# In the last network, sums of two products go to SBUF, and ScalarE squares the positive parts while it rounds them

## The chip, the cores and the metric

The kernel runs on one NeuronCore of one Trainium2 chip. Its engines have an instruction queue each and work through it in order: TensorE (matmuls, into PSUM), VectorE, ScalarE, GpSimd and SyncE; the profile calls them PE, DVE, ACT, POOL and SP. An instruction waits at the head of its queue until the instructions of other engines that it needs have signalled. The metric is the device time of one execution in microseconds. The kernel before takes 709.72 us (median of 3 runs, 708.33 to 710.09).

## The reference

Three networks run one after another on 1152 tokens of 512 values, all in 32-bit floats: causal attention with a bias (2 batches, 8 heads, 576 positions), a mixture of four ReLU networks (weights of 512 x 1024 and 1024 x 512 each), and a last network with a squared ReLU:

```python
# the four experts, then the last network
for e in range(E):
    h = np.maximum(x @ w1[e], 0.0)
    out += p[:, e:e + 1] * (h @ w2[e])
...
h = x @ w_in          # (1152, 512) @ (512, 2048)
r = np.maximum(h, 0.0)
g = r * r
return (g @ w_out).astype(np.float32)
```

## The kernel before

Each matmul is made in three parts: a value x is split into hi, x rounded to the matmul format fp32r, and lo, x minus hi, and the products hi*hi, hi*lo and lo*hi are added up in PSUM. So each value that goes into a matmul costs an instruction that rounds it and one that subtracts.

The code at hand is the long stage that makes the second to fourth expert and the last network. It runs over 20 pieces of hidden columns (q, 0 to 19; four for each 1024 columns; q from 12 on is the last network) and two blocks of tokens (b: 512 tokens as two halves of 256, 640 tokens as two halves of 320). One call of `group` handles one q and one b; there are 40, and they are numbered here from 0 in the order of the list `groups` (L1125). Group 24 is the first of the last network, group 26 is piece 12 with the tokens of 320 columns a half, group 27 piece 13 with the same tokens.

A group makes its four quarters of hidden values (j is the half of the columns, half the half of the tokens) from seven block products instead of eight (Winograd's form of Strassen's method). The products are made in the order 1, 2, 6, 5, 7, 4, 3, each by six matmuls (`product`, L1017). Products 1, 6, 7 and 4 add up in one PSUM bank, pa, and between them ScalarE copies the running sum out into SBUF (`keep`, L1064: tiles u1 and u2). Product 2 has the bank pb. Products 5 and 3 share one bank, pc, one after the other. pa and pb change places from group to group, and pc is a single bank for all groups.

`hidden(j, half, ps, kept)` (L1069) makes a quarter out of a bank and a kept sum. VectorE adds the two: for j = 0 in place, in the bank, for j = 1 into the kept tile. For q below 12 ScalarE then writes hi with a Relu, and VectorE writes lo with one scalar_tensor_tensor (positive part minus hi). In the last network the value is squared, with four instructions in turn: ScalarE's Relu into a tile r (L1081), VectorE's scalar_tensor_tensor r = max(x, 0) * r (L1082), which reads x again, ScalarE's copy of r to hi (L1083), and VectorE's r minus hi to lo (L1084). The bank is free when the last of these that reads x is done.

`y_unit` (L1035) is the second matmul of the network: for one tile of 128 tokens, six matmuls of 512 columns, out of a group's hi and lo. The units of a group are issued in between the products of the next one, so that TensorE has work while the other engines make hidden values. After every second piece VectorE adds the bank of a tile to the accumulator in SBUF (L240, L242).

Between the products, `do_next` also issues other work: sums and splits of the weights (`w_pair`, L943; ScalarE's copies L970, L971, L985 and L992, GpSimd's differences L79), and the decoding of the last network's weights, which arrive in another number format (`decode`, L120): ScalarE's L132, GpSimd's L134, then five instructions on VectorE, L141, L145, L147, L149 and L150, and a store.

The order in each engine's queue isn't the order of this code: a scheduler sets it when the program is built, by its own estimate of when each instruction can start. So the change of one buffer or one instruction can move many others. Tiles come from pools with a number of buffers (`bufs`): a new tile of a name waits until all use of the one that had its buffer is over.

Of the kernel before, what the change touches and what calls it, by code (L numbers as in the profile page):

```python
# [8 lines left out]
F32 = mybir.dt.float32  # L9
F32R = mybir.dt.float32r  # L10
U32 = mybir.dt.uint32
AF = mybir.ActivationFunctionType
ALU = mybir.AluOpType
# [3 lines left out]
P = 128  # L17
# [3 lines left out]
E = 4  # L21
# [27 lines left out]
def fused_kernel(ctx, tc, qk, v, s, dp, w1, w2, wi, wo, out):  # L49
# [5 lines left out]
    nc = tc.nc  # L55
# [130 lines left out]
    def ph_tile():  # L186
        pool = ph_pools[ph_count[0] % len(ph_pools)]
        ph_count[0] += 1
        return pool.tile([P, 512], F32, tag="ph", name="ph")
# [76 lines left out]
    class Unit:  # L266
        def __init__(self, b, h, q0, q1, group, slot):
            self.b, self.h, self.q0, self.q1 = b, h, q0, q1
            self.group, self.slot = group, slot
            kt = KT[b]  # L270
            self.tiles = [i for i in range(5) if kt[i] >= q0 and kt[i + 1] <= q1]
# [29 lines left out]
    with tc.tile_pool(name="att", bufs=2) as att, tc.tile_pool(name="atc", bufs=1) as const_a:  # L301
# [107 lines left out]
        for u in units:  # L409
            for i in u.tiles:  # L410
                t = Step()
# [464 lines left out]
    str_p = ctx.enter_context(tc.tile_pool(name="str", bufs=1))  # L876
# [140 lines left out]
    def product(ps, i, q, b, first):  # L1017
        wn, xn = PRODUCT[i]
        n = BLOCKS[b][1]
        s, c0, stride = W_AT[wn]  # L1020
        m = 0
        for k2 in range(2):
            for wh, xx in ((0, 0), (0, 1), (1, 0)):
                c = c0 + k2 * stride
                nc.tensor.matmul(  # L1025
                    ps[:, :n],
                    lhsT=pw[q][s][:, wh, c : c + P],
                    rhs=x_part(b, xn, xx, k2),
                    start=(first and m == 0),
                    stop=(m == 5),  # L1030
                    skip_group_check=True,
                )
                m += 1
# [19 lines left out]
    def group(q, b, turn, do_next):  # L1053

        n = BLOCKS[b][1]
        hs = [str_p.tile([P, 2, 640], F32R, tag="h", name="h", bufs=4) for _ in range(2)]
        free = [ph_tile(), ph_tile()]  # L1060
        pa, pb = free if turn else free[::-1]
        pc = pc_p.tile([P, 512], F32, tag="y", name="pc")

        def keep(ps, name):  # L1064
            t = str_p.tile([P, 320], F32, tag=name, name=name, bufs=1)
            nc.scalar.copy(t[:, :n], ps[:, :n])  # L1066
            return t

        def hidden(j, half, ps, kept):  # L1069
            x = ps[:, :n]  # L1070
            if kept is not None:
                x = kept[:, :n] if j else x
                nc.vector.tensor_tensor(x, ps[:, :n], kept[:, :n], op=ALU.add)
            cols = slice(half * n, half * n + n)
            hi, lo = (hs[j][:, i, cols] for i in range(2))
            if q < E * 4 - 4:
                nc.scalar.activation(hi, x, AF.Relu)
                nc.vector.scalar_tensor_tensor(lo, x, 0.0, hi.bitcast(F32), op0=ALU.max, op1=ALU.subtract)  # L1078
                return
            r = str_p.tile([P, 320], F32, tag="r", name="r", bufs=2)[:, :n]  # L1080
            nc.scalar.activation(r, x, AF.Relu)  # L1081
            nc.vector.scalar_tensor_tensor(r, x, 0.0, r, op0=ALU.max, op1=ALU.mult)  # L1082
            nc.scalar.copy(hi, r)  # L1083
            nc.vector.tensor_tensor(lo, r, hi.bitcast(F32), op=ALU.subtract)  # L1084

        product(pa, 1, q, b, True)
        p1 = keep(pa, "u2")
        product(pb, 2, q, b, True)
        hidden(0, 0, pb, p1)
        do_next(0)  # L1090
        product(pa, 6, q, b, False)
        u1 = keep(pa, "u1")
        product(pc, 5, q, b, True)
        do_next(1)
        product(pa, 7, q, b, False)
        u2 = keep(pa, "u2")
        hidden(1, 1, pc, u2)
        do_next(2)
        product(pa, 4, q, b, False)
        hidden(1, 0, pa, None)  # L1100
        do_next(3)
        product(pc, 3, q, b, False)
        hidden(0, 1, pc, u1)
        do_next(4)
        t0 = BLOCKS[b][0] // P
        order = range(t0, t0 + 2 * n // P)
        if (q + 2) // 4 == E - 1 and (q + 2) % 4 < 2:
            order = LAST[b]
        return [lambda t=t: y_unit(q, b, t, hs) for t in order]
# [72 lines left out]
    for i, (q, b) in enumerate(groups):  # L1182
        todo = units
        n_units, n_side = len(todo), len(side[i])
        done = [0, 0]

        def do_next(k):

            upto = min(n_units, k if n_units == 4 and k == 3 else k + 1)
            while done[0] < upto:  # L1190
                todo[done[0]]()
                done[0] += 1
            while done[1] < n_side * (k + 1) // 5:
                side[i][done[1]]()
                done[1] += 1
            for op in extra[i, k]:
                op()

        units = group(q, b, i % 2, do_next)
# [50 lines left out]
```

## Time and profile before

| | |
|---|---|
| median of 3 runs | 709.72 us (708.33 to 710.09) |
| the profiled execution | 707.28 us, its span 705.5 us |
| TensorE busy | 685.7 us (97%), 4164 matmuls |
| VectorE busy | 500.9 us (71%) |
| ScalarE busy | 353.1 us (50%) |
| GpSimd busy | 315.3 us (45%) |
| chain that ended last | TensorE 76%, VectorE 14% |
| first and last squared Relu of the last network (L1081) | 500.1 and 694.5 us |
| granted clock of TensorE | 1.00 in every stretch from 100 to 650 us |

The times of the trace are microseconds from the start of the span. The stage with the groups begins at about 210 us, the last network at about 498 us. A row of a timeline gives an instruction's start and its length; a bracket says how long the engine had been idle before it and which instruction ended that. Rows of several equal instructions are merged with a count. For TensorE the ends of matmuls are modelled, so two of them overlap in the listing: how long a block takes is read from the distance of its start to the next one's.

### The profile page before, as it was taken

What the parts mean: (1) busy time and instruction counts of PE and PEld (TensorE: products, weight loads), DVE (VectorE), ACT (ScalarE), POOL (GpSimd) and SP (SyncE); (2) the same over time, 40 slices, a digit from 0 to 9 for tenths busy, and PEclk for the clock granted to TensorE, in tenths of its full rate; (3) what the DMA queues carried; (4) which work ended last, traced back from release to release, by engine and by line L of the source; (5) the groups of instructions that cost most, each with busy time, mean ns of one, the idle gap of its engine ahead of it and who ended that gap; (6) DMA issues with size and microseconds to landing.
All of it is one profiled execution on the core that took longest, in us unless ns stands there. A gap on an engine that the chain in (4) does not pass through costs nothing.

```text
span 705.5 us, 11939 instructions
## 1 busy us (share of the span) xinstructions
PE 685.7 (97%) x4164; PEld 598.1 (85%) x4164; DVE 500.9 (71%) x1142; ACT 353.1 (50%) x880; POOL 315.3 (45%) x332
## 2 busy tenths in 40 slices
PE   9889999999999999999999999999998999999997
PEld 8668787778998989889989899889997888899996
DVE  5986677751668657887787887869588789955464
ACT  7976776651355343352533433535574445535341
POOL 5754454420073583591770943812438726704000
PEclk9999999999999999999999999999999999999999
DMA  7652333100141234243343433431203332300012
GB/s 224 201 154 77 104 86 86 36 1 1 60 148 36 75 116 140 100 150 120 121 154 115 134 121 119 150 120 46 60 31 106 96 120 83 103 18 1 1 60 75
DMA packets 37060, 66.17 MB, mean 94 GB/s; under 512 B 4392, under 2 KB 12232, under 8 KB 37000
## 3 DMA queue, kind: packets, MB, share of 16 engines
q1 hardware_dynamic: 27784, 40.23, 19.1%
q10 hardware_dynamic: 9216, 25.17, 10.7%
q8 instruction: 33, 0.54, 0.3%
q14 instruction: 27, 0.22, 0.1%
HBM read 52.73 MB, written 10.82 MB: 90 GB/s over the span
## 4 chain that ended last, share of the span: by engine, by line
PE 76%; DVE 14%; issue 4%; ACT 3%; POOL 1%; ACTq 0%; DVEq 0%; POOLq 0%
PE y L1043 26%; PE ph L1025 16%; PE ph L197 7%; PE pc L1025 7%; PE y L223 6%; PE o L616 4%; PE pt L559 3%; DVE dy L145 3%; DVE raw_d L149 2%; PE s L463 2%; DVE raw_d L141 2%; PE s L464 1%; PE idle L337 1%; DVE h L1078 1%; ACT w L992 1%
## 5 line engine op out<-in xcount | busy, mean ns | idle before, releaser
L1043 PE MATMUL y<-w,h 128*128 128x512 f32 x1080 | 276.3, 392 | 0.0
L1043 PEld LDWEIGHTS y<-w,h 128*128 128x128 f32 x1080 | 193.9, 188 | 30.9
L1025 PE MATMUL ph<-tx,w 128*128 128x256 f32 (+1 forms) x720 | 115.4, 296 | 0.1
L1025 PEld LDWEIGHTS ph<-tx,w 128*128 128x128 f32 x720 | 106.2, 189 | 7.6 <-ACT u L1066 0.9
L1066 ACT COPY u<-ph 128x256 f32<-128x256 f32 (+1 forms) x120 | 47.7, 397 | 94.8 <-PE ph L1025 93.0
L79 POOL TENSOR_TENSOR w<-raw_w,w 128x512 fp32r<-128x512 f32 x58 | 80.7, 1405 | 18.1 <-ACT w L992 18.1
L1025 PE MATMUL pc<-xh,w 128*128 128x256 f32 (+1 forms) x320 | 78.4, 300 | 6.6 <-DVE r L1082 3.1
L1025 PE MATMUL ph<-xh,w 128*128 128x256 f32 (+1 forms) x320 | 77.9, 298 | 1.3 <-DVE h L1078 0.8
L79 POOL TENSOR_TENSOR w<-val,w 128x512 fp32r<-128x512 f32 x40 | 58.7, 1483 | 43.8 <-ACT w L985 43.8
L519 POOL TENSOR_SCALAR p<-p,stat 128x128 f32<-128x128 f32 (+9 forms) x80 | 47.7, 608 | 56.3 <-DVE stat L514 21.4
L134 POOL TENSOR_SCALAR dy<-dy 128x512 f32<-128x512 f32 x32 | 19.9, 622 | 114.8 <-ACT dy L132 107.5
L1025 PEld LDWEIGHTS pc<-xh,w 128*128 128x128 f32 x320 | 56.0, 188 | 11.2 <-DVE r L1082 4.6
L1025 PEld LDWEIGHTS ph<-xh,w 128*128 128x128 f32 x320 | 56.0, 188 | 4.5 <-DVE h L1078 1.5
L197 PE MATMUL ph<-xh,w 128*128 128x256 f32 (+1 forms) x256 | 58.3, 301 | 0.1
L223 PE MATMUL y<-w,h 128*128 128x512 f32 x216 | 57.4, 396 | 0.0
L501 ACT ACTIVATE p<-p,stat 128x384 f32<-128x384 f32 (+9 forms) x80 | 46.6, 583 | 18.8 <-DVE stat L487 15.9
L1025 PE MATMUL ph<-xl,w 128*128 128x256 f32 (+1 forms) x160 | 47.4, 297 | 0.0
L1025 PE MATMUL pc<-xl,w 128*128 128x256 f32 (+1 forms) x160 | 47.3, 296 | 0.0
L487 DVE CUSTOM_DVE_ANT_0 p<-s,mask 128x448 f32<-128x448 f32 (+8 forms) x72 | 33.1, 462 | 19.4 <-PE pt L559 12.2
L1084 DVE TENSOR_TENSOR h<-r,h 128x256 fp32r<-128x256 f32 (+1 forms) x64 | 36.1, 567 | 13.9 <-ACT h L1083 12.5
L197 PEld LDWEIGHTS ph<-xh,w 128*128 128x128 f32 x256 | 43.3, 188 | 1.6 <-DVE h L211 0.4
L223 PEld LDWEIGHTS y<-w,h 128*128 128x128 f32 x216 | 38.9, 188 | 6.0
(149 smaller groups left out, 1273.2 us busy)
## 6 DMA issues: line engine op xcount, KB each, us to landing
raw_w<-in_w SPq DMA_DIRECT2D x64, 256.0 KB
raw_d<-in_wi ACTq DMA_DIRECT2D x16, 512.0 KB
staged<-dy ACTq DMA_DIRECT2D x32, 256.0 KB
raw_d<-in_wo ACTq DMA_DIRECT2D x16, 512.0 KB
raw_w<-staged SPq DMA_DIRECT2D x32, 256.0 KB
raw<-in_qk SPq DMA_DIRECT2D x40, 144.0 KB
v<-in_v SPq DMA_DIRECT2D x8, 256.0 KB
out<-acc_a SPq DMA_DIRECT2D x6, 256.0 KB
```

The lines of the kernel that those rows point to most:

```text
L79: eng.tensor_tensor(out_, a, b.bitcast(F32), op=ALU.subtract)
L145: nc.vector.scalar_tensor_tensor(top, top, 0x80000000, high, op0=ALU.bitwise_and, op1=ALU.bitwise_or)
L197: nc.tensor.matmul(ps[:, :n], lhsT=w1_ap(e, wh, kk, f), rhs=x[:, kk, t0 : t0 + n], start=(i == 0), stop=(i == 3 * KD - 1),)
L223: mm = nc.tensor.matmul(ps, lhsT=h[:, hh, o : o + P], rhs=w2_ap(e, wh, f), start=(f == 0 and i == 0), stop=(f == NF - 1 and i == 2),)
L487: t.red = nc.vector.tensor_tensor_reduce(t.p[: t.n, a:z], ps[: t.n, : z - a], t.bias[:, a:z], scale=-0.125, scalar=init, op0=ALU.add, op1= ...
L501: t.exp = nc.scalar.activation(t.p[: t.n, : t.w], t.p[: t.n, : t.w], AF.Exp, bias=t.nmax, scale=-1.0, accum_out=t.st[: t.n, 4 + t.c : 5 + ...
L519: norm = nc.gpsimd.tensor_scalar(t.p[: t.n, : t.w], t.p[: t.n, : t.w], t.st[: t.n, 6 + t.c : 7 + t.c], 1.0, op0=ALU.mult, op1=ALU.mult)
L616: return nc.tensor.matmul(u.o[i * D : (i + 1) * D, qs - u.q0 : u.nq], lhsT=vv[:kn, j, i * D : (i + 1) * D], rhs=rhs, start=(j == 0), stop= ...
L1025: nc.tensor.matmul(ps[:, :n], lhsT=pw[q][s][:, wh, c : c + P], rhs=x_part(b, xn, xx, k2), start=(first and m == 0), stop=(m == 5), skip_gr ...
L1043: nc.tensor.matmul(ps, lhsT=hs[j][:, hh, o : o + P], rhs=wt[e, 2, g][:, wh, j * DM : (j + 1) * DM], start=(g % 2 == 0 and i == 0 and j == ...
L1066: nc.scalar.copy(t[:, :n], ps[:, :n])
L1084: nc.vector.tensor_tensor(lo, r, hi.bitcast(F32), op=ALU.subtract)
```

## The change

Three things change in `group`, the first two only in the last network (`late`) except for the number of buffers.

- The sum of product 3 and u1 (half 1, j = 0) goes into the kept tile u1, not back into the bank; the sum of product 2 and the first kept sum (half 0) stays in its bank as before, and that of product 5 and u2 goes to u2 as before. For half 1 the squares are then made in the kept tile itself; for half 0 in the tile r.
- ScalarE writes hi as the Square of r, straight after its Relu; VectorE then makes r * r, both inputs from r, instead of max(x, 0) * r, and subtracts hi.
- u1 has two buffers instead of one, for all groups, and r one instead of two. The four tiles take the same space as before.

```diff
--- before.py
+++ after.py
@@ -1061,26 +1061,32 @@
         pa, pb = free if turn else free[::-1]
         pc = pc_p.tile([P, 512], F32, tag="y", name="pc")
 
+        def kept_tile(name):
+            bufs = 2 if name == "u1" else 1
+            return str_p.tile([P, 320], F32, tag=name, name=name, bufs=bufs)[:, :n]
+
         def keep(ps, name):
-            t = str_p.tile([P, 320], F32, tag=name, name=name, bufs=1)
-            nc.scalar.copy(t[:, :n], ps[:, :n])
+            t = kept_tile(name)
+            nc.scalar.copy(t, ps[:, :n])
             return t
 
         def hidden(j, half, ps, kept):
+            late = q >= E * 4 - 4
             x = ps[:, :n]
             if kept is not None:
-                x = kept[:, :n] if j else x
-                nc.vector.tensor_tensor(x, ps[:, :n], kept[:, :n], op=ALU.add)
+
+                x = kept if (half if late else j) else x
+                nc.vector.tensor_tensor(x, ps[:, :n], kept, op=ALU.add)
             cols = slice(half * n, half * n + n)
             hi, lo = (hs[j][:, i, cols] for i in range(2))
-            if q < E * 4 - 4:
+            if not late:
                 nc.scalar.activation(hi, x, AF.Relu)
                 nc.vector.scalar_tensor_tensor(lo, x, 0.0, hi.bitcast(F32), op0=ALU.max, op1=ALU.subtract)
                 return
-            r = str_p.tile([P, 320], F32, tag="r", name="r", bufs=2)[:, :n]
+            r = x if half else kept_tile("r")
             nc.scalar.activation(r, x, AF.Relu)
-            nc.vector.scalar_tensor_tensor(r, x, 0.0, r, op0=ALU.max, op1=ALU.mult)
-            nc.scalar.copy(hi, r)
+            nc.scalar.activation(hi, r, AF.Square)
+            nc.vector.tensor_tensor(r, r, r, op=ALU.mult)
             nc.vector.tensor_tensor(lo, r, hi.bitcast(F32), op=ALU.subtract)
 
         product(pa, 1, q, b, True)
```

With it the scheduler's order changes, from group 10 on. The three places below are those that the prediction speaks of.

VectorE, groups 11 and 12 (the experts, where the code of a group is as before). L1073, in the new file L1079, is the add of `hidden`; L1078, L1084 in the new file, makes lo; L238 adds to an accumulator; L141 to L149 are decoding. `pc_4124` is group 11's bank pc. Before:

```order
L141 TENSOR_SCALAR raw_d_4088<-dy_4200 128x512
L1073 TENSOR_TENSOR pc_4124<-pc_4124,u1_4155 128x320
L145 SCALAR_TENSOR_TENSOR dy_4200<-dy_4200,raw_d_4088 128x512
L147 TENSOR_SCALAR raw_d_4088<-dy_4200 128x512
L1073 TENSOR_TENSOR ph_4249<-ph_4249,u2_4258 128x256
L149 SCALAR_TENSOR_TENSOR raw_d_4088<-raw_d_4088 128x512
L1078 SCALAR_TENSOR_TENSOR h_4120<-pc_4124,h_4120 128x320
```

Now:

```order
L1079 TENSOR_TENSOR pc_4124<-pc_4124,u1_4155 128x320
L141 TENSOR_SCALAR raw_d_4088<-dy_4200 128x512
L1084 SCALAR_TENSOR_TENSOR h_4120<-pc_4124,h_4120 128x320
L145 SCALAR_TENSOR_TENSOR dy_4200<-dy_4200,raw_d_4088 128x512
L1079 TENSOR_TENSOR ph_4249<-ph_4249,u2_4258 128x256
L238 SCALAR_TENSOR_TENSOR acc_a_75<-y_4142,pn_74,acc_a_75 128x512
L238 SCALAR_TENSOR_TENSOR acc_a_75<-y_4163,pn_74,acc_a_75 128x512
```

The instruction that makes lo out of `pc_4124`, the last that reads the bank, stood behind L141, L145, L147 and L149, and now stands behind L141 alone.

VectorE, group 26. `pc_6109`, now `pc_6105`, is its bank pc, and the add into u2 is that of product 5. Before:

```order
L141 TENSOR_SCALAR raw_d_5493<-dy_6200 128x512
L145 SCALAR_TENSOR_TENSOR dy_6200<-dy_6200,raw_d_5493 128x512
L147 TENSOR_SCALAR raw_d_5493<-dy_6200 128x512
L149 SCALAR_TENSOR_TENSOR raw_d_5493<-raw_d_5493 128x512
L1073 TENSOR_TENSOR u2_6172<-pc_6109,u2_6172 128x320
L150 TENSOR_TENSOR dy_6200<-dy_6200,raw_d_5493 128x512
L1082 SCALAR_TENSOR_TENSOR r_6175<-u2_6172,r_6175 128x320
L1082 SCALAR_TENSOR_TENSOR r_6193<-ph_6108,r_6193 128x320
```

Now (L1079 is the add, L1089 r * r, L1090 makes lo):

```order
L141 TENSOR_SCALAR raw_d_5493<-dy_6195 128x512
L145 SCALAR_TENSOR_TENSOR dy_6195<-dy_6195,raw_d_5493 128x512
L147 TENSOR_SCALAR raw_d_5493<-dy_6195 128x512
L149 SCALAR_TENSOR_TENSOR raw_d_5493<-raw_d_5493 128x512
L150 TENSOR_TENSOR dy_6195<-dy_6195,raw_d_5493 128x512
L1079 TENSOR_TENSOR u2_6168<-pc_6105,u2_6168 128x320
L1079 TENSOR_TENSOR u1_6139<-pc_6105,u1_6139 128x320
L1089 TENSOR_TENSOR u2_6168<-u2_6168 128x320
```

The fifth step of the decoding, L150, stood behind the add into u2 and now stands ahead of it; the two adds follow each other.

ScalarE, same place. `r_6193`, now `r_6188`, is the tile r of product 4 of group 26. Before (L1081 Relu, L1083 copy to hi):

```order
L1081 ACTIVATE r_6193<-ph_6108 128x320
L970 CAST w_6351<-raw_w_6224 128x256
L155 DMA staged5121_6320<-dy_6200 128x512
L1083 CAST h_6106<-r_6175 128x320
L1066 COPY u2_6244<-ph_6235 128x320
L126 DMA raw_d_6322<-in_wo 128x1024
L1083 CAST h_6106<-r_6193 128x320
L132 ACTIVATE dy_6324<-raw_d_5619 128x512
L971 CAST w_6351<-raw_w_6226 128x512
L985 CAST w_6352<-val_6345 128x512
L985 CAST w_6352<-val_6346 128x512
```

Now (L1087 Relu, L1088 Square to hi):

```order
L1088 ACTIVATE h_6102<-u2_6168 128x320
L1087 ACTIVATE r_6188<-ph_6104 128x320
L132 ACTIVATE dy_6317<-raw_d_5619 128x512
L970 CAST w_6344<-raw_w_6218 128x256
L971 CAST w_6344<-raw_w_6220 128x512
L985 CAST w_6345<-val_6338 128x512
L985 CAST w_6345<-val_6339 128x512
L1088 ACTIVATE h_6102<-r_6188 128x320
```

The step that writes hi for product 4 came ahead of L132, L971 and both L985, and now comes behind them and L970.

TensorE, the end of the program. The last `ph` and `pc` rows are products 4 and 3 of group 39; the y tiles fed by `h_7749` and `h_7750`, now `h_7719` and `h_7720`, are that group's. Before:

```order
L1025 MATMUL ph_7751<-tx14_2486,w_7353 128x320 x6
L1025 MATMUL pc_7753<-xh_72,w_7354 128x320
L1025 MATMUL pc_7753<-xl_73,w_7354 128x320
L1025 MATMUL pc_7753<-xh_72,w_7354 128x320 x2
L1025 MATMUL pc_7753<-xl_73,w_7354 128x320
L1025 MATMUL pc_7753<-xh_72,w_7354 128x320
L1043 MATMUL y_7853<-w_7254,h_7642 128x512
L1043 MATMUL y_7774<-w_7494,h_7749 128x512 x3
L1043 MATMUL y_7795<-w_7494,h_7749 128x512 x3
L1043 MATMUL y_7774<-w_7494,h_7750 128x512 x2
L1043 MATMUL y_7795<-w_7494,h_7750 128x512 x2
```

Now:

```order
L1043 MATMUL y_7744<-w_7469,h_7719 128x512 x3
L1043 MATMUL y_7765<-w_7469,h_7719 128x512 x3
L1025 MATMUL ph_7721<-tx14_2486,w_7331 128x320 x6
L1025 MATMUL pc_7723<-xh_72,w_7332 128x320
L1025 MATMUL pc_7723<-xl_73,w_7332 128x320
L1025 MATMUL pc_7723<-xh_72,w_7332 128x320 x2
L1025 MATMUL pc_7723<-xl_73,w_7332 128x320
L1025 MATMUL pc_7723<-xh_72,w_7332 128x320
L1043 MATMUL y_7744<-w_7469,h_7720 128x512 x2
L1043 MATMUL y_7765<-w_7469,h_7720 128x512 x2
L1043 MATMUL y_7744<-w_7469,h_7720 128x512
```

Two tiles' three matmuls each of group 39 and the last one of group 38 stood behind products 4 and 3; now the six stand ahead of them, and what follows product 3 at once reads `h_7720`, the half of the columns that product 4 makes.

## Rows read from the trace of the kernel before

**Rows 1.** The page, busy time of each engine:

```profile
PE 685.7 (97%) x4164; PEld 598.1 (85%) x4164; DVE 500.9 (71%) x1142; ACT 353.1 (50%) x880; POOL 315.3 (45%) x332
```

**Rows 2.** Timeline of TensorE: start, us, instruction; in brackets idle time before, releaser:

```profile
356.57 0.39 PE L1025 MATMUL pc<-xh,w 128*128 128x256 f32 x1 [0.51 <-DVE h L1078]
...
535.76 0.42 PE L1025 MATMUL pc<-xh,w 128*128 128x320 f32 x1 [1.22 <-DVE u L1073]
...
537.30 0.41 PE L1025 MATMUL ph<-xh,w 128*128 128x320 f32 x1 [0.39 <-DVE r L1082]
...
541.05 0.41 PE L1025 MATMUL pc<-xh,w 128*128 128x320 f32 x1 [0.34 <-DVE r L1082]
...
555.78 0.39 PE L1025 MATMUL pc<-xh,w 128*128 128x256 f32 x1 [1.19 <-DVE r L1082]
...
568.74 0.39 PE L1025 MATMUL pc<-xh,w 128*128 128x256 f32 x1 [1.52 <-DVE r L1082]
...
575.29 0.28 PE L1025 MATMUL pc<-xh,w 128*128 128x256 f32 x1
```

**Rows 3.** Timeline of VectorE, 351.7 to 356.5, groups 11 and 12:

```profile
351.75 0.48 DVE L1073 TENSOR_TENSOR pc<-pc,u 128x320 f32<-128x320 f32 x1
352.15 1.38 DVE L145 SCALAR_TENSOR_TENSOR dy<-dy,raw_d 128x512 uint32<-128x512 uint32 x1
...
356.04 0.48 DVE L1078 SCALAR_TENSOR_TENSOR h<-pc,h 128x320 fp32r<-128x320 f32 x1
```

**Rows 4.** Timeline of VectorE, 530.2 to 536.5, group 26:

```profile
530.23 0.69 DVE L240 COPY acc_a<-y 128x512 f32<-128x512 f32 x1 [0.17 <-PE y L1043]
530.83 1.31 DVE L141 TENSOR_SCALAR raw_d<-dy 128x512 uint32<-128x512 uint32 x1
...
534.21 1.10 DVE L149 SCALAR_TENSOR_TENSOR raw_d<-raw_d 128x512 f32<-128x512 uint32 x1
535.23 0.48 DVE L1073 TENSOR_TENSOR u<-pc,u 128x320 f32<-128x320 f32 x1
535.63 0.81 DVE L150 TENSOR_TENSOR dy<-dy,raw_d 128x512 f32<-128x512 f32 x1
```

**Rows 5.** Timeline of ScalarE, 536.4 to 540.2:

```profile
536.44 0.40 ACT L970 CAST w<-raw_w 128x256 fp32r<-128x256 f32 x1
...
537.92 0.68 ACT L132 ACTIVATE dy<-raw_d 128x512 f32<-128x512 f32 x1
538.50 0.60 ACT L971 CAST w<-raw_w 128x512 fp32r<-128x512 f32 x1
539.01 1.14 ACT L985 CAST w<-val 128x512 fp32r<-128x512 f32 x2
```

**Rows 6.** Chain of waits, in order of time: start, us, what:

```profile
651.88 0.72 PE pc L1025 x6
...
692.07 0.88 PE ph L1025 x6
...
693.82 7.06 PE y L1043 x31
```

**Rows 7.** Groups by line and form, 498 to 697: busy, mean ns, idle; then ScalarE's timeline:

```profile
L1084 DVE TENSOR_TENSOR h<-r,h 128x320 fp32r<-128x320 f32 x32 | 22.1, 693 | 10.5 <-ACT h L1083 9.7
...
L1083 ACT CAST h<-r 128x320 fp32r<-128x320 f32 x32 | 14.6, 460 | 12.0 <-DVE r L1082 11.9
...
L1082 DVE SCALAR_TENSOR_TENSOR r<-ph,r 128x320 f32<-128x320 f32 x16 | 7.8, 488 | 11.9 <-ACT r L1081 11.8
...
693.04 0.44 ACT L1081 ACTIVATE r<-ph 128x320 f32<-128x320 f32 x1 [2.72 <-PE ph L1025]
```

**Rows 8.** Busy us (PE, PEld, DVE, ACT, POOL) of two stretches; a group of the second:

```profile
550.00:600.00 50.00, 47.28 (x275) 42.21 (x274) 44.24 (x77) 25.62 (x61) 27.91 (x25) 1.00 0.35 107
650.00:697.00 47.00, 47.00 (x272) 42.35 (x271) 25.32 (x54) 17.63 (x43) 0.00 (x0) 1.00 0.06 23
...
L1084 DVE TENSOR_TENSOR h<-r,h 128x320 fp32r<-128x320 f32 x8 | 3.9, 490 | 2.3 <-ACT h L1083 2.1
```

## The prediction

> **What bounds the kernel now.** I read the busy line of the page first [rows 1]: TensorE is busy 685.7 of 705.5 us, so everything else is a question of when TensorE waits. The change moves no matmul: both programs issue the same 4164. So it can win only TensorE's idle time and lose only by making new idle time. The second view is TensorE's timeline, searched for rows with an idle time in brackets [rows 2]. The new order of instructions differs from the old one only from group 10 on (330 us of the trace), and from there to the end the idle places are: 0.51 us at 356.57, the same again at 404.51 and 452.45 (it is a repeating pattern), one wait on the way to 462, and in the last network 1.22, 0.39 and 0.34 us around group 26 (535.76 to 541.05), 1.19 at 555.78 and 1.52 at 568.74. In the last network that is 4.66 us, all of it behind VectorE. After an idle time the first matmul lasts 0.39 us in [rows 2] instead of 0.28 (the row at 575.29), so I count 0.11 us more for each.
>
> The places differ. At 356.57, 555.78 and 568.74 product 5 of a group wants the single pc bank, and VectorE has not yet finished reading it for the group before: the instruction that frees it stands behind the steps of the weight decoding in VectorE's queue. [rows 3] show it for 356.57: the add on pc starts at 351.75, but the last reader of the bank starts at 356.04, with decoding steps of up to 1.38 us between. At 535.76 the wait is for the add itself: [rows 4] show it starting at 535.23, behind four decoding steps that began at 530.83.
>
> For lengths I use [rows 6]: six matmuls of 256 columns take 0.72 us, six of 320 take 0.88, a y matmul 7.06/31 = 0.228.
>
> **The change part by part.** *Sums to SBUF.* In the last network the sum of product 3 leaves pc for the u1 tile, so pc is free after the add and no longer after add, Relu and VectorE's second read. [rows 3] show the distance in the older form that the middle network keeps (the add over at 352.23, the last reader at 356.5); at 555.78 and 568.74 the wait is for the same second read, so both go: 1.19 + 1.52 + 2 x 0.11 = 2.93 us won. *What is late next:* the new order puts product 5 earlier behind product 3, since the bank is expected back sooner. Between product 3 of group 27 and product 5 of group 29 it holds 9 products and 36 y matmuls, 9 x 0.72 + 36 x 0.228 = 14.7 us. VectorE has 23 instructions there, the freeing add last: five decoding steps (from 530.83 to 536.44 with 0.40 for the add between them, 5.2, [rows 4]), five copies of y at 0.69 (3.4), three adds of 0.45, five multiplications (two at 0.49, three at about 0.42) and five differences (two of them at 0.69, [rows 7]): about 14.9 us. That is level. Bounds: nothing (the steps overlap a little at their ends), or all 2.93 back. I take 1.0 us lost over groups 28 to 30, nearer to level.
>
> *A second u1 tile, one r tile.* A kept tile now stays in use until the difference is done, so the copy of a group's first product into u2 waits for the half (1,1) of the group before. That copy has 6 to 9 us of other matmuls in front of its use in the new order; behind it on ScalarE stand the Square of the half (0,1) and the next group's first Relu, which the y matmuls want 3 us later. I cost it at 0, and at 0.4 us for small waits in groups 29 to 36, where product 4 is followed by the next product into its bank after only 0.72 us and the Relu that frees it starts 0.1 us after it (692.07 + 0.88 against 693.04) and lasts 0.44 ([rows 6, 7]); bounds 0 and 1.5 (ten such places of 0.15).
>
> *ScalarE squares.* Instead of Relu, VectorE, copy, VectorE the chain is Relu, Square on ScalarE, then two on VectorE. The counts on both engines stay. Square isn't in the trace; I take it as long as the Relu on the same shape (0.44, [rows 7]), bounds 0.40 and 0.60 (a cast of the 512 wide tile, [rows 5]). It is hidden: the y matmuls of a half come at least 1.6 us after its last product in the new order, and Relu plus Square is 1.0, except at two places.
>
> *Group 26.* In the new order of VectorE the fifth decoding step stands ahead of the add, not behind it. The add starts 0.80 us later than at 535.23 (the fifth step's 0.81, [rows 4]), and product 3 waits 2.02 instead of 1.22 us: 0.80 lost. Product 2 of group 27 then needs the Relu of product 4, which now stands behind Relu and Square of the other half: 3 x 0.44 = 1.3 us after product 3's start against 0.88 of cover, about as long as the 0.39 recorded before. Then the first y matmuls of group 26 need the Square of product 4, which the new order of ScalarE puts behind five steps for the weights: by the starts in [rows 5] 0.58 + 0.40 + 0.51 + 1.14, and 0.46 for itself (a cast of 320 columns, [rows 7]), 3.1 us after that Relu, so 4.4 us after product 3's start. TensorE is there after 1.35 + 0.88 + 0.88 = 3.1: 1.3 lost, and the 0.34 of 541.05 goes. Net 0.80 + 1.3 - 0.34 = 1.76 lost. Bounds: -1.95 (all three waits go, if decoding starts earlier by as much) and +3.
>
> *The tail.* Before, the last two products are followed by one y matmul of group 38 and six of group 39 that need neither of them. Now those six stand ahead of the products, and the y matmuls right behind product 3 need the Square of product 4: 0.1 + 0.44 + 0.46 = 1.0 us after product 4, with 0.88 of cover; four matmuls later they need its difference, which sits on VectorE behind the add of product 3: 2.45 us after product 4 against 2.0. Lost 0.15 + 0.45 = 0.6; the second chain, for product 3, is covered by the six matmuls between.
>
> *The middle network.* Only u1's second tile and the scheduler's choice act here; at the places at 356.57 and 452.45 the instruction that frees pc now stands behind one decoding step instead of three. Both waits go: 2 x (0.51 + 0.11) = 1.24 won. The one at 404.51 keeps its order.
>
> *The multiplication.* It replaces a read of PSUM by a second read of SBUF. [rows 7] show what that does beside GpSimd: the difference, with two SBUF inputs, takes 0.693 us on average in this network, the scalar_tensor_tensor on the same shape out of PSUM 0.488; where GpSimd is idle (650 to 697, [rows 8]) the difference takes 0.490. So of the 64 multiplications the 48 that read PSUM before may be stretched, the 24 of 320 columns by 0.20 each, 4.9 us of VectorE's time. In the worst stretch VectorE is busy 44.24 of 50 us [rows 8]. I hold most of it as hidden there; a part is in the 1.0 us above. The Trainium skill, "SBUF — State Buffer", section "Who interferes with whom", says that a VectorE instruction with two SBUF inputs contends with a GpSimd instruction that reads SBUF, and one with at most one does not: by it this change puts 48 instructions into contention. The trace agrees (0.693 against 0.488), and no row shows whether one tile read as both inputs counts as two; if it does not, the 4.9 us falls away.
>
> **Sum:** -2.93 + 1.0 + 0.4 + 1.76 + 0.6 - 1.24 = -0.41 us. The profiled execution took 707.28 us (span 705.5, 1.8 around it), so 706.9 by its own measure; the median of the runs is 709.72, 2.44 above that execution, and I carry the difference over: **709.3 us**.
>
> **Rivals.** *The covers hold* (faster): group 26 loses nothing and VectorE keeps pace. For it speaks that ScalarE and VectorE no longer hand a tile back and forth: the wait at 537.30 in [rows 2] is for a product on VectorE that itself needed ScalarE. Then all 4.66 us of the last network go with 5 x 0.11, 1.24 in the middle, and the tail costs 0.6: -5.85, 703.9 us. Against it speaks the order around group 26.
>
> *GpSimd's reads hold VectorE* (slower): the 4.9 us of stretched multiplications lie where VectorE feeds TensorE. It decides once VectorE's idle time of 5.8 us in 550 to 600 no longer covers the waits that it has for ScalarE. If half of it reaches TensorE, the time is 709.3 + 2.45 = 711.8; if all, 714.2. Against it: after 650 us GpSimd does nothing, and the chain has fewer steps that hand over between engines.
>
> *New waits cancel the old ones exactly* is the forecast itself, by the sum above.
>
> **How the numbers follow.** A measurement of this kernel can tell about 0.3%, 2.1 us, from no change. The forecast has a chance of 0.55 with its own range of 707 to 711.6, the covers that hold 0.25, GpSimd's hold 0.20. Faster by over 0.3%: 0.25 and an eighth of the forecast's, 0.32. Slower: most of 0.20 and a little of the forecast's, 0.22. Same: 0.46. The range reaches into both rivals: 704.2 to 713.
>
> **What would show it.** Right: TensorE's idle rows at 555.78, 568.74, 356.57 and 452.45 are gone; around group 26 product 3 still waits, for the add, by about 2 us, and a y matmul waits for ScalarE's Square; a y matmul waits near the end; the multiplications of 320 columns average well above 0.49. Wrong: no idle time at group 26, or TensorE's idle sum in the last network above 6 us, or a wait for a copy into u2.

## The result and the profile after

The changed kernel takes 714.74 us (median of 7 runs, 713.16 to 717.64), the kernel before 709.75 on the same chip (7 runs, 708.33 to 712.38): ratio 1.0065, 95% interval 1.0047 to 1.0084, so 0.65% slower. The forecast was no change, 709.3, range to 713.0.

First the page's line of busy times, beside [rows 1]:

```profile
PE 690.6 (97%) x4164; PEld 600.4 (84%) x4164; DVE 505.4 (71%) x1142; ACT 354.9 (50%) x880; POOL 314.8 (44%) x332
```

VectorE and TensorE are busy longer with as many instructions. Where TensorE waits now, from its timeline (start, length, instruction, idle time before it and what ended that), answering [rows 2]:

```profile
535.58 0.41 PE L1025 MATMUL pc<-xh,w 128*128 128x320 f32 x1 [1.64 <-DVE u L1079]
...
561.23 0.96 PE L1043 MATMUL y<-w,h 128*128 128x512 f32 x3 [1.18 <-DVE h L1090]
...
593.19 1.01 PE L1043 MATMUL y<-w,h 128*128 128x512 f32 x3 [1.80 <-DVE h L1090]
...
613.26 0.98 PE L1043 MATMUL y<-w,h 128*128 128x512 f32 x3 [1.22 <-DVE h L1090]
...
645.29 0.73 PE L1043 MATMUL y<-w,h 128*128 128x512 f32 x2 [0.96 <-DVE h L1090]
...
703.75 0.98 PE L1043 MATMUL y<-w,h 128*128 128x512 f32 x3 [0.16 <-DVE h L1090]
```

The rows at 356.57, 452.45, 555.78 and 568.74 of before are gone, as forecast. In their place the y matmuls, which before waited for nothing of the kind, wait five times for L1090, the difference that makes lo: 5.3 us together. With the shorter waits the last network has 8.5 us of idle time, where it had 4.66.

Why lo is late shows in VectorE's timeline ahead of the wait at 613.26:

```profile
606.75 1.59 DVE L1089 TENSOR_TENSOR r<-r 128x320 f32<-128x320 f32 x1 [0.41 <-ACT h L1088]
608.37 1.47 DVE L1090 TENSOR_TENSOR h<-r,h 128x320 fp32r<-128x320 f32 x1
609.76 1.52 DVE L141 TENSOR_SCALAR raw_d<-dy 128x512 uint32<-128x512 uint32 x1
```

and GpSimd's at the same time:

```profile
606.70 1.29 POOL L79 TENSOR_TENSOR w<-raw_w,w 128x512 fp32r<-128x512 f32 x1
607.95 3.04 POOL L79 TENSOR_TENSOR w<-val,w 128x512 fp32r<-128x512 f32 x2
```

r * r starts 0.05 us after GpSimd's first difference and takes 1.59 us, the difference behind it 1.47. GpSimd's two rows are one instruction of 1.29 and two of 1.52 back to back; VectorE's three end 0.3 to 0.4 us behind the ends of these, one by one. The wait at 613.26 is ended by a later difference, that of u1 (612.20, 1.01 us), which stands behind these three and two more. At 645.29 the wait is for such a pair itself, which ends at 645.24:

```profile
642.23 1.51 DVE L1089 TENSOR_TENSOR r<-r 128x320 f32<-128x320 f32 x1 [0.28 <-ACT h L1088]
643.78 1.46 DVE L1090 TENSOR_TENSOR h<-r,h 128x320 fp32r<-128x320 f32 x1
```

By the form of the instructions, from 498 to 697 us (busy, mean ns, idle time before), answering [rows 7]:

```profile
L1090 DVE TENSOR_TENSOR h<-r,h 128x320 fp32r<-128x320 f32 x15 | 12.5, 836 | 0.4
L1089 DVE TENSOR_TENSOR r<-r 128x320 f32<-128x320 f32 x15 | 11.7, 780 | 5.4 <-ACT h L1088 5.4
L1090 DVE TENSOR_TENSOR h<-u,h 128x320 fp32r<-128x320 f32 x14 | 9.7, 694 | 0.3
L1089 DVE TENSOR_TENSOR u<-u 128x320 f32<-128x320 f32 x14 | 8.5, 606 | 5.5 <-ACT h L1088 5.5
...
L1089 DVE TENSOR_TENSOR r<-r 128x256 f32<-128x256 f32 x16 | 7.8, 485 | 0.3 <-ACT h L1088 0.3
```

and from 650 us, where GpSimd has 2.8 us of work left, the answer to [rows 8]:

```profile
L1089 DVE TENSOR_TENSOR r<-r 128x320 f32<-128x320 f32 x4 | 2.0, 489 | 2.7 <-ACT h L1088 2.7
```

So one tile read as both inputs is stretched beside GpSimd like a difference of two tiles: 0.78 us on average, up to 1.59, against 0.49 without GpSimd.

At group 26 the Square of product 4 stands where the forecast put it on ScalarE, behind five steps for the weights:

```profile
536.44 0.42 ACT L1087 ACTIVATE r<-ph 128x320 f32<-128x320 f32 x1
...
539.17 0.48 ACT L1088 ACTIVATE h<-r 128x320 fp32r<-128x320 f32 x1
```

It ends at 539.65, 4.07 us after product 3 starts (4.4 forecast). But no y matmul waits for it: TensorE gets there only at 540.22, since it runs the products behind its wait at half clock. In three stretches (the length, then PE, PEld, DVE, ACT and POOL busy, the granted clock, DMA's share and GB/s):

```profile
533.00:536.40 3.40, 1.76 (x11) 1.50 (x11) 2.49 (x3) 0.81 (x2) 2.62 (x3) 1.00 0.12 43
536.80:540.00 3.20, 3.09 (x11) 3.10 (x12) 1.96 (x4) 3.20 (x9) 2.49 (x3) 0.50 0.50 156
541.00:544.00 3.00, 3.00 (x18) 2.62 (x17) 2.97 (x4) 1.12 (x3) 3.00 (x3) 1.00 0.37 100
```

The granted clock is 0.50, the 1.2 GHz level, right behind the idle time at 535.58, and 1.00 again from 541. The same happens from 594.8, behind the 1.80 us at 593.19, and at 120, in the attention, which the change doesn't touch:

```profile
120.40:123.60 3.20, 3.20 (x18) 1.91 (x15) 0.92 (x4) 1.57 (x4) 0.60 (x2) 0.50 0.17 53
...
595.00:598.00 3.00, 3.00 (x13) 2.81 (x13) 2.72 (x4) 0.00 (x0) 2.38 (x3) 0.50 0.03 11
```

So the profiled execution (715.17) stands 7.9 us above that of before (707.28), the medians only 5.0. Clock alone is not the difference: the changed kernel's executions with a mean clock of 0.998 and 0.999 took 713.28 and 713.16, and those of before with 0.998 to 1.0, beside later runs, 707.7 to 711.0.

### The profile page after: what moved, and what is told of

It reads as the page before. It is cut to its first block, busy times and chain, and to the rows that moved or that the text cites. A ratio compares the mean times of both kernels' runs of the same rounds, so it can differ in the third digit from the quotient of the medians.

```text
span 713.3 us, 11904 instructions
## 1 busy us (share of the span) xinstructions
PE 690.6 (97%) x4164; PEld 600.4 (84%) x4164; DVE 505.4 (71%) x1142; ACT 354.9 (50%) x880; POOL 314.8 (44%) x332
## 4 chain that ended last, share of the span: by engine, by line
PE 80%; DVE 11%; ACT 2%; issue 2%; DMA 2%; SPq 1%; POOL 1%; ACTq 0%; DVEq 0%; POOLq 0%
PE y L1043 30%; PE ph L1025 19%; PE pc L1025 8%; PE ph L197 7%; PE y L223 6%; PE o L616 4%; PE pt L559 3%; PE s L463 2%; DVE dy L145 1%; PE s L464 1%; DVE raw_d L149 1%; DVE h L1090 1%; DVE r L1089 1%; DVE raw_d L141 1%; DMA raw_w<-in_w 1%
## 5 line engine op out<-in xcount | busy, mean ns | idle before, releaser
L1079 DVE TENSOR_TENSOR u<-pc,u 128x256 f32<-128x256 f32 (+1 forms) x56 | 25.3, 452 | 47.1 <-ACT u L1070 32.6
```

What stands on the lines that cost most here:

```text
L1079: nc.vector.tensor_tensor(x, ps[:, :n], kept, op=ALU.add)
```

## The experiments

Theory A: GpSimd's reads of SBUF stretch the added multiplications and what stands behind them on VectorE, and y matmuls wait for lo. Theory B: the order of instructions that the scheduler made for the change loses the time. Theory C: the stretches at half clock do. Every run is compared with the kernel before, timed beside it; changes below are by these ratios. Nearly all orders are the scheduler's own; "held" versions get an order-only edge between each two neighbours on an engine, so that their order is that of the kernel named.

**GpSimd without its weight differences, in both programs.**

```diff
-            less(nc.gpsimd, t[:, 1, n], wraw.pop((e, 2, g, half)), t[:, 0, n])
+            if q >= 14:
+                wraw.pop((e, 2, g, half))
+                nc.gpsimd.memset(t[:, 1, n].bitcast(F32), 0.0)
+            else:
+                less(nc.gpsimd, t[:, 1, n], wraw.pop((e, 2, g, half)), t[:, 0, n])
```

The same is done in `sum_lo` of `w_pair` (not shown). It takes in the pieces 14 to 19, all of the last network but its first two; GpSimd's other work, sums of two tiles among it, stays.

> The changed kernel, but GpSimd's weight differences in the last eight groups' worth of work (from the fifteenth network index on, which takes in the last network) become memsets of zero: the lo parts of those weights are left out, so the output is not the reference's. GpSimd then writes SBUF there and reads none. The changed kernel took 714.7 us against 709.7 before. Theory A (GpSimd's SBUF reads stretch the new r*r and the differences, and y matmuls wait for the differences): r*r of 320 columns falls from 0.78 to about 0.5 us, the y waits for the difference (5.3 us in all) go, time 708.5 to 710. Theory B (the tighter order of instructions loses it whatever the durations are): r*r may get shorter, but 3 us or more of the y waits stay and the time is 713 or more. Theory C (the loss is TensorE's stretches at half clock, three of them new): as B, unless the idle time ahead of the two late ones goes; then about 712.

> The kernel before with the same memsets in place of GpSimd's weight differences (the same lo parts left out). It says what GpSimd's reads cost the program before, so that the pair of these two shows the change without them. Theory A: before loses little to GpSimd, 708 to 710, and the changed kernel with memsets lies within 1.5 us of it on either side. Theory B: the pair stays 4 to 5.5 us apart, as the two kernels are now.

Measured: 706.12 (ratio 0.9967, 0.9954 to 0.998) and 704.54 (0.9937, 0.9921 to 0.9953). Beside its 1.0065 the changed kernel gains 1.0% (7 us), the kernel before 0.6% (4.5). Both came out below what theory A had said: GpSimd's differences cost the kernel before more than expected. The same with the orders held:

> The changed kernel with GpSimd's weight differences from the fifteenth piece on (counted from 0: pieces 14 to 19) replaced by memsets of zero, as in the run before (the lo parts of those weights are left out), but every engine's instruction order is held to that of the changed kernel by order-only edges. Only what GpSimd does in its places is different. The free order with memsets took 706.1 us, the changed kernel 714.7. Theory A (contention with GpSimd's reads): the order does not matter much, 706 to 708.5. Theory B (the order that the scheduler made): 712 to 715, since the order is the same. In between, the distance to 714.7 is what the contention costs in this order and the distance to 706.1 what the order costs.

> The kernel before with the same memsets (the same lo parts left out), every engine held to the order of the kernel before. The free order with memsets took 704.5 us, the kernel before 709.1 beside it. Theory A: what GpSimd's reads cost the kernel before in its own order is small, since only the 32 differences and 16 of the multiplications have two SBUF inputs: 707 to 709. Theory B: 708.5 to 710, no contention to remove.

Measured: 706.45 (0.996, 0.9946 to 0.9973) and 705.09 (0.995, 0.993 to 0.997). That is 1.05% (7.5 us) for the changed kernel and 0.5% (3.5 us) for the one before, where 707 to 709 had been expected. The two programs, 0.65% apart with GpSimd's reads, are 0.1% apart in their held orders and 0.3% in the free ones, each with an interval of about 0.2% either way. TensorE's waits from 330 us on in the held version of the changed kernel (us, times, longest):

```profile
PE y L1057 <- ACT h L1102: 1.7, 3, 0.8
PE pc L1039 <- DVE u L1093: 0.8, 1, 0.8
...
PE y L1057 <- DVE h L1104: 0.2, 1, 0.2
```

By form in that version, from 498 to 697 us:

```profile
L1103 DVE TENSOR_TENSOR r<-r 128x320 f32<-128x320 f32 x16 | 11.6, 725 | 6.1 <-ACT h L1102 6.0
L1104 DVE TENSOR_TENSOR h<-r,h 128x320 fp32r<-128x320 f32 x16 | 8.2, 515 | 0.4
```

The y waits for lo, 5.3 us, are down to 0.2 with TensorE, VectorE and ScalarE in the same order. The multiplications of r fell less than expected, from 0.78 to 0.725 us and not to 0.5 (some still meet GpSimd's other work); the differences behind them fell from 0.836 to 0.515. A memset is also shorter than the difference it replaces (0.53 us against 1.4), which this test doesn't take apart; but from 495 us on neither VectorE nor TensorE waits for GpSimd in the changed kernel. Theory B alone, and an order that is bad whatever the durations, falls. The granted clock is 1.00 in every window from 498 to 697 us: the late half-clock stretches went with the idle time ahead of them, so C is a consequence. The memsets, which only write, stretch nothing here: five differences of 320 columns lie wholly beside one and take 0.48 or 0.49 us each.

The reverse test came out empty:

> The changed kernel, nothing left out, GpSimd reading as ever, but with the orders of TensorE, VectorE and ScalarE that the scheduler made for the version with memsets (held by order-only edges on TensorE and VectorE; ScalarE's comes out the same). Theory A: GpSimd's reads are back, so 712 to 715. Theory B: the order was the trouble, so 706 to 709, and this would be a version that beats the kernel before without any change of work.

Measured: 713.18 (1.0068, 1.0045 to 1.009). The two orders turned out to differ in only a few rows on VectorE and ScalarE, so this is the changed kernel once more. It serves as a control: with the edges on TensorE and VectorE the ratio is 1.0068, without them 1.0065, so holding an order costs nothing that shows.

**Only the inputs of the multiplication, orders held.** In the changed kernel the second SBUF input is taken away:

```diff
-            nc.vector.tensor_tensor(r, r, r, op=ALU.mult)
+            nc.vector.tensor_scalar(r, r, 1.0, None, op0=ALU.mult)
```

> The changed kernel in its own order, held, with r * r replaced by a multiplication of r by the constant 1, which has one SBUF input instead of two (the square is left out of what lo is made from). GpSimd reads as ever, and the differences keep two inputs. Theory A: these 64 no longer stretch (0.49 us or less instead of 0.78 for 320 columns), and two thirds of the y waits go; 709 to 712. Theory B: 713.5 to 715. If it comes out at or below 709, the second input of r * r alone was the loss.

Measured: 710.28 (1.0011, 0.9995 to 1.0028), 0.5% of the time back. The y waits for lo fall from 5.3 to 2.5 us, by half and not by two thirds. The instruction with one input isn't free of GpSimd either (whole last network, then from 650 us):

```profile
L1096 DVE TENSOR_SCALAR r<-r 128x320 f32<-128x320 f32 x15 | 8.5, 565 | 6.0 <-ACT h L1095 6.0
...
L1096 DVE TENSOR_SCALAR r<-r 128x320 f32<-128x320 f32 x4 | 1.3, 323 | 2.8 <-ACT h L1095 2.8
```

It takes 0.32 us alone and 0.57 on average here, so part of the gain is that it is shorter, and how much isn't shown. The cleaner test is to put the 48 instructions into the kernel before, in its order, with nothing else:

```diff
-            nc.vector.scalar_tensor_tensor(r, x, 0.0, r, op0=ALU.max, op1=ALU.mult)
+            nc.vector.tensor_tensor(r, r, r, op=ALU.mult)
```

> The kernel before, every engine held to its order, with only VectorE's scalar_tensor_tensor (positive part of the PSUM sum times r) replaced in place by r * r out of SBUF: 48 more instructions with two SBUF inputs, nothing else moved, and the banks free a step earlier. Theory A (the count of such instructions is the loss): 712 to 714, 3 to 4 us slower. Theory B (the order is the loss): 708 to 710.5, no change, and the r * r may be stretched without anybody waiting.

Measured: 712.8 (1.0046, 1.0028 to 1.0064): 3.3 us slower, 2.0 to 4.5, as theory A has it. Groups by form from 498 to 697 us, beside the 488 ns of the replaced instruction in [rows 7]:

```profile
L1089 DVE TENSOR_TENSOR r<-r 128x320 f32<-128x320 f32 x30 | 24.9, 839 | 10.3 <-ACT r L1088 10.2
L1091 DVE TENSOR_TENSOR h<-r,h 128x320 fp32r<-128x320 f32 x30 | 20.9, 703 | 8.6 <-ACT h L1090 8.2
```

TensorE's largest wait there:

```profile
PE y L1050 <- ACT h L1090: 4.8, 4, 2.1
```

The differences keep their mean (703 against 693), the multiplications go from 0.49 to 0.84, and since in this program ScalarE's copy to hi waits for the product, the y matmuls wait for hi. In the changed kernel hi doesn't need the product, so the 3.3 us are the price in this order and not a share of the changed kernel's loss.

**Parts of the change, each in an order of its own.** Half 0 squared out of PSUM again (`if half: r * r; else: scalar_tensor_tensor(r, x, 0.0, r, ...)`):

> The changed kernel, but for the half whose sum stays in PSUM (products 2 and 4, 32 of the 64) VectorE makes the square from the PSUM bank and r, as the kernel before does; the other 32 multiply the SBUF tile by itself. Theory A: half of the stretched instructions read one SBUF input again and take about 0.49 instead of 0.78 us; some half of the loss comes back, 711 to 713, and the y waits for the difference of half 0 go while those of half 1 stay. Theory B: no change against the changed kernel, 714 to 715.5.

Only the sums and buffers (half 0 squared out of PSUM as in the version above, and `nc.scalar.copy(hi, r)` behind the multiplication in place of Square):

> The part of the change that sends the sum of half 1 to SBUF, with its buffers, but with ScalarE's copy of the finished square instead of its Square: half 0 squares out of PSUM as before, half 1 multiplies the SBUF tile by itself. 96 instructions with two SBUF inputs. Theory A: 16 more than before cost 16 x 0.08 = 1.3 us, and the two waits of product 5 for the bank (2.9 us) may go; 708 to 711. Theory B (the order that the scheduler makes decides): anywhere from 706 to 716, out of line with the count.

Only the buffers (`bufs=2` for u1, 1 for r, in the kernel before):

> The kernel before with only the buffers of the change: two for u1 and one for r. 80 instructions with two SBUF inputs. Theory A: no more contention; r's single buffer makes the Relu of the next half wait for the difference of the one before; 709 to 712. It also shows what the shorter waits in the experts' part (2 x 0.6 us forecast) are worth by themselves, if its order there is that of the changed kernel. Theory B: out of line with the count.

Only the Square (`nc.scalar.activation(hi, r, AF.Square)` ahead of VectorE's multiplication, no copy):

> The kernel before with only its copy to hi replaced by a Square of r straight after the Relu; sums, buffers and VectorE's multiplication out of PSUM as before. 80 instructions with two SBUF inputs, as before. Theory A: no more contention than before, and the chain of a half loses one hand-over; 707.5 to 710. Theory B: out of line with the count.

Measured: 718.11 (1.0123, 1.0106 to 1.0141), 714.16 (1.0058, 1.0042 to 1.0074), 714.27 (1.0065, 1.0045 to 1.0085) and 718.64 (1.0115, 1.0097 to 1.0133). All four miss what theory A said by the count of instructions: none adds more than 16 with two SBUF inputs to those of before, and all are as slow as the whole change or slower. So a version in a new order can lose several us here without the added instructions; the new buffers alone lose as much as the whole change. Two of them were run again with memsets, orders held, to see whether it does so by itself:

> The version with only the buffers changed (714.3 us), held to its order, with memsets in place of GpSimd's weight differences in pieces 14 to 19 (the lo parts of those weights are left out). If its loss of 4.6 us is its order's meeting with GpSimd's reads: 705 to 707. If it is waits that the order makes by itself: 709 to 711.

> The version with only ScalarE's Square (718.6 us), held to its order, with the same memsets. If its loss of 9 us is its order's meeting with GpSimd's reads: 705 to 708. If it is waits that the order makes by itself: 712 to 715.

Measured: 706.22 (0.9941, 0.9922 to 0.996) and 712.66 (1.0042, 1.0025 to 1.006). The order with only the buffers changed costs nothing without GpSimd's weight differences. That with only the Square keeps some 0.9% over the kernel before without them; its largest wait is there with and without the reads. TensorE's timeline of the Square alone:

```profile
544.03 2.07 PE L1043 MATMUL y<-w,h 128*128 128x512 f32 x4 [2.83 <-ACT h L1082]
```

and of the held version with memsets:

```profile
540.16 1.88 PE L1057 MATMUL y<-w,h 128*128 128x512 f32 x4 [2.95 <-ACT h L1096]
```

This is the wait that the forecast had put into group 26 of the changed kernel: y for a Square that stands too far back on ScalarE.

**Taking the squares off VectorE.** In the changed kernel, and then in the kernel before with its own sums and buffers:

```diff
             nc.scalar.activation(hi, r, AF.Square)
-            nc.vector.tensor_tensor(r, r, r, op=ALU.mult)
+            nc.scalar.activation(r, r, AF.Square)
```

> The changed kernel, but ScalarE squares r in place as well (a second Square), so that VectorE's 64 multiplications are gone and only the differences stay with two SBUF inputs. Theory A: with some 38 us taken off VectorE the y waits for the difference go nearly all; 32 more ScalarE instructions per half-set of about 0.45 us are covered except around group 26 and the tail; 706 to 710. Theory B: the chain of a half is as long as before (one Square in place of the multiplication) and the order as tight: 713 to 716.

> The kernel before with both squares on ScalarE (Square to hi and Square in place), no multiplication on VectorE, sums and buffers as before, in an order of its own. 64 instructions with two SBUF inputs, as in the version with both squares on ScalarE that took 704.9. Theory A: 704 to 708, the sums in SBUF matter little. Theory B: it can come out anywhere from 703 to 716. If it lies below 704.9, the sums in SBUF cost something even there.

Measured: 704.86 (0.9946, 0.9927 to 0.9965) and 705.45 (0.9945, 0.9924 to 0.9966). Both beat the kernel before by 0.55%, some 3.9 us, with GpSimd reading as ever. The first came out below its range (706 to 710). Its differences are stretched as much as in the changed kernel (those of r; 0.550 for those of u1 and u2, 0.694 there), and TensorE waits only 0.4 us for them; group by form and TensorE's waits from 330 us:

```profile
L1090 DVE TENSOR_TENSOR h<-r,h 128x320 fp32r<-128x320 f32 x16 | 13.4, 835 | 6.5 <-ACT r L1089 6.2
```

```profile
PE y L1043 <- DVE acc_a L242: 1.7, 1, 1.7
...
PE y L1043 <- DVE h L1090: 0.4, 2, 0.2
```

A stretched difference is the only VectorE step of its chain then, not the second of two. The second version has neither the sums in SBUF nor the new buffers and gains as much, so the sums weren't needed for it. Both run in orders of their own, so how much of the 0.55% is the order's isn't shown. One more step, Relu and Square of half 0 written into the PSUM bank (`r = x`), so that only 32 differences have two SBUF inputs:

> The version with both squares on ScalarE (704.9 us), but for half 0 the Relu and the second Square write the PSUM bank in place of the tile r, so that the difference of half 0 has one SBUF input and the bank is held until the difference is done. Instructions with two SBUF inputs in the last network: 128 in the changed kernel, 80 before, 64 with both squares on ScalarE, 32 here. Theory A (each such instruction costs its share: the 48 that the change added cost 3.9 us, 0.08 each): 702.5 to 704, unless the longer hold of a bank makes TensorE wait. A rival for this version: the bank is held by two ScalarE steps and one of VectorE more, about 1.4 us, and products 2 and 1 of the next group wait; 706 to 712.

Measured: 713.99 (1.0053, 1.0038 to 1.0068); the rival was right. VectorE's instructions are stretched least of all versions with GpSimd's reads (19 us in all over the shortest of each form, the kernel before 21, the changed one 29), and TensorE waits for the bank instead:

```profile
565.00 0.98 PE L1025 MATMUL ph<-tx,w 128*128 128x256 f32 x6 [2.89 <-ACT u L1070]
```

## Why the prediction was wrong

**The step that failed** is "I hold most of it as hidden there; a part is in the 1.0 us above", on the multiplications that lose their PSUM input. It was a little low at the instruction and wrong at TensorE. The 32 multiplications of 320 columns average 0.693 us now ((780 + 606)/2) against 0.488, so they are stretched by 32 x 0.205 = 6.6 us, where the forecast had 24 x 0.205 = 4.9. That the meeting with GpSimd reaches TensorE is what the memsets show: without GpSimd's weight differences the 0.65% between the two kernels (4.6 us) shrinks to 0.1% in held orders and 0.3% in free ones. In the order of before, where only the multiplications were changed, they cost 3.3 us (2.0 to 4.5). What misled me was the cover: I read VectorE's busy share of 44.24 of 50 us [rows 8] as room. After the change VectorE is idle longer in that stretch:

```profile
550.00:600.00 50.00, 46.71 (x265) 41.33 (x264) 42.19 (x73) 23.47 (x56) 25.81 (x24) 0.97 0.33 106
```

Yet TensorE waits. A share over 50 us doesn't say what one chain takes: where r * r and the difference both meet GpSimd, they take 1.59 + 1.47 = 3.1 us instead of 1.0, and at 645.29 the y matmuls stand right behind such a pair. The rival "GpSimd's reads hold VectorE", at 0.20, came nearest: all of the stretch, 714.2. That this lies so near the 714.74 is in part luck, since it counts the multiplications alone and has the rest of the sum at -0.41. The point at which I let it decide (VectorE's idle time in 550 to 600 used up) was the wrong one; the other signs of being wrong, an idle sum above 6 us (8.5) and a wait for the copy into u2, did show. Nor had I priced the differences, which keep their form: at 320 columns they average 0.765 us ((836 + 694)/2) against 0.693, 32 x 0.07 = 2.3 us more.

**Waits removed:** right. Product 5 no longer waits at 555.78 and 568.74, nor at 356.57 and 452.45. The buffers alone do the last two: their version is, like the changed kernel, busy on TensorE for 167.49 of the 168 us from 330 to 498, the kernel before for 165.60.

**Backlog in groups 28 to 30, 1.0 us:** the queue was late, but the wait fell on y (1.18 at 561.23) and not on the bank.

**Group 26:** the add was late (1.64 for product 3, 2.02 forecast). The Square's place and time were right, the wait for it was hidden by TensorE's half clock: by an estimate from the 0.88 us of a block in [rows 6], TensorE would otherwise have come at 536.91 + 2 x 0.88 = 538.67, 1.0 us before the Square's end. The version with the Square alone shows the wait itself.

**The Square and the copies:** the Square of 320 columns averages 0.47 us, 0.44 assumed. The copy into u2, costed at 0, kept product 1 waiting for 0.52 us at 532.79 and 0.32 at 620.34; with 0.4 for such small waits the sum was off by 0.4 there.

**The tail, 0.6 us:** 0.16 at 703.75 is what the trace shows, and it waits for the difference, as said.

**What the sum had left** without GpSimd's weight differences: the forecast was -0.41 us, and by the ratios it is +0.7 in the held pair and +2.1 in the free one, each within some 1.6 us either way. So apart from GpSimd's weight differences the sum was about right, perhaps one or two us too low.

**What stays open.** GpSimd's weight differences cost the kernel before some 3.5 us in its order, the changed kernel 7.5, the order with only new buffers some 9, though that has no more instructions with two SBUF inputs than before. So a part of the price is which instructions meet in an order, not how many could. The 48 multiplications account for 3.3 us in the order of before; how the changed kernel's loss splits between them and the order that lets VectorE's instructions meet GpSimd's was not settled. A version of the changed kernel in its own order with half 0 squared out of PSUM, which would have told more, wasn't run, nor was the kernel before with r * r and memsets.

## What to carry to other kernels

When an edit moves an operand from PSUM to SBUF on VectorE, look at what GpSimd reads at that moment, and count the stretch into the latency of the chain that TensorE waits for, not into a busy share. Where two VectorE steps follow each other in such a chain, try moving one to an engine that isn't touched: ScalarE's Squares of 320 columns took 0.47 us before 650 us, beside GpSimd's work, and 0.47 after. Two Squares on ScalarE won 0.55% where the change, with one Square and a multiplication, lost 0.65%, each in an order of its own. And in a program whose order a scheduler sets, compare variants with the order held: four partial edits, each in an order of its own, missed what the count of instructions gave by 2 to 9 us and told little until then.

## What the runs showed of the hardware

- One tile given as both inputs of a VectorE instruction counts as two SBUF inputs beside GpSimd: 0.78 us on average and up to 1.59, against 0.49. The Trainium skill, "SBUF — State Buffer", section "Who interferes with whom", says that a VectorE instruction with two SBUF inputs contends with a GpSimd instruction that reads SBUF, and not with one that only writes it. The traces agree with both: 1.59 us beside a difference, 0.48 or 0.49 beside a memset.
- A tensor_scalar with a single SBUF input, 0.32 us for 320 columns alone, averages 0.57 in the last network and takes up to 1.40 beside GpSimd's weight differences. The Trainium skill, "SBUF — State Buffer", section "Who interferes with whom", says that tensor_scalar can contend in its two-port modes, and that a VectorE instruction with at most one SBUF input doesn't contend outside these modes, a condition that the prediction leaves out. The trace agrees that it can contend; which mode it ran in no run here shows.
- TensorE's granted clock was 0.50 from 536.8 to 540 and from 595 to 598 us, behind idle times of 1.6 and 1.8 us that ended on VectorE, and then 1.00 again; where that idle time was taken away, it stayed at 1.00. Not every such wait brings it: the version of before with r * r has one of 2.1 us and a mean clock of 0.999.
